# Reordered first units, earlier weight loads, regrouped first output pieces and filler matmuls in a recurrence + soft-MoE kernel

## The chip, the cores and the metric

The kernel runs on one core of one Trainium2 chip. The metric is the device time of one execution in microseconds (us); the median of 13 runs of the kernel before is 205.56 us. Times inside an execution come from one profiled run and are counted from the start of its span.

## What is computed

The input is a sequence tensor of 4 batches, 5056 steps and 256 channels. First a gated linear recurrence runs over the steps of each batch; then a soft mixture of experts (MoE) with 8 experts of 4 slots each mixes all 20224 tokens. Cut to what matters:

```python
sig = 1.0 / (1.0 + np.exp(-f_logit))
f = lower_bound + (1.0 - lower_bound) * sig
for t in range(S):                       # per batch and channel
    h = f[:, t] * h + (1.0 - f[:, t]) * x[:, t]
    y[:, t] = h
# y becomes x of shape (20224, 256)
logits = x @ phi                         # 32 slots
d = softmax of logits over tokens;  slot_input = d.T @ x
for e in range(8):                       # w1: 256 x 1024, w2: 1024 x 256
    slot_out[e] = np.maximum(slot_input[e] @ w1[e], 0.0) @ w2[e]
c = softmax of logits over slots;  out = c @ slot_out
```

So nothing can be written out before the last step of the recurrence has fed the slots and all expert weights have been used.

## The kernel before, in words

**Units.** The work is cut into 40 units: 10 groups of 512 steps times 4 batches, unit n being group n // 4 of batch n % 4. The load of a unit is 512 KB of `f_logit` and 512 KB of `x`, both float32. The expert weights are 16 further loads (8 of w1, 8 of w2), cast to bf16 on the way, issued one by one by `load_w` (L118) from GpSimd's queue; L120 is w1, L122 is w2. In the profile all of these weight tiles are called w_sb.

**Stages of a unit.** `load` (L162) puts f and x of a unit into buffers of the pool `ld`, which holds three pairs of units of each. `gate` (L180) is the sigmoid on ScalarE, f_t to s_t (L188). `enter` (L190) multiplies s_t and x_t into u_t on GpSimd (L199; unit 0 on VectorE, L195). `s_to_channels` and `u_to_channels` (L216, L222) transpose both on TensorE into PSUM tiles sp and up (L214; L208 and L211 in the odd group 8). `decay` (L230) turns sp into the factors a on ScalarE (L237). `scan` (L241) is the recurrence on VectorE, two instructions of L247 per unit. `to_tokens` (L252) transposes h back (L258, tile hp), and `keep_tokens` (L268) copies it to ht (L272), on VectorE for even n and on ScalarE for odd n. Per group, `logits`, `exps` (with two activation table loads), `weights_to_tokens` and `slots` follow.

**Order.** The scheduler is off (`tc.manual_schedule()`, L132): every engine executes its instructions in the order in which the Python program emits them, and waits in place for what it needs. The main loop (L408) runs n from 0 to 39 and emits stages of several units per step: in the first units (n < 4) the gate of unit n+3, the decay of n+2, and the scan of n; from n = 4 on, on even n, the gate of n+4 and n+5 in one instruction, and on odd n the decay of n+1 and n+2. `W_AT` (L130) is a table from n to the number of weight loads emitted in that step, right after `enter(n + 3)` on GpSimd.

**Limits on buffers.** sp has one PSUM buffer (a pair of units), hp one, up two. A transpose into sp for the next pair waits for the decays of the pair before; `to_tokens(n)` waits for `keep_tokens(n - 1)`, and what is behind it on TensorE waits too. A load waits until its buffer has been read by the gate (f) or by enter (x).

**The experts.** When the slots are summed, sin (L521, L522) goes through w1 (L539), Relu, a transpose, and w2. Experts 0 to 3 share one pass (L575). Experts 4 to 7 are the loop over j at L583: eight matmuls (L585) each, which need the weights w2[4 + j]; after j = 0, the earlier experts' sum is added (L590) and the row sums of groups 4 to 9 are taken (L319, L322) into one half of a PSUM tile called tail. Four reciprocals (L598) follow in VectorE's order, then slot_out (L599). `spin(dst, k)` (L125) emits k matmuls of 512 columns whose result nobody uses; the kernel before has seven of them elsewhere.

**The output.** Each of 41 output units (40, and one for the odd ends of group 8) is made of matmuls into a PSUM tile op (L622), a scaling into ob by VectorE (`by_vector`, L628) or ScalarE (`by_scalar`, L633), and a write issued from SyncE's queue. op has four row blocks of 256 float32[...]. The first two units are split over both engines (L646 to L652): unit 0 into four pieces of 128 KB, unit 1 into two of 256 KB; the others are written whole (L660).

Of the kernel before, what the change touches and what calls it, by code (L numbers as in the profile page):

```python
# [18 lines left out]
def kernel(  # L19
# [10 lines left out]
    nc = tc.nc  # L30
# [8 lines left out]
    R = 4  # L39
    G = P * R  # L40
    n_grp = (S + G - 1) // G
    n_unit = n_grp * B
# [84 lines left out]
            nc.tensor.matmul(dst, w1_sb[0][:, 0, :P], w1_sb[0][:, 0, :G],  # L127
                             start=True, stop=True, skip_group_check=True)

    W_AT = {12: 1, 18: 1, 24: 1, 29: 1, 32: 1, 33: 1, 34: 3, 35: 1, 36: 6}  # L130
    w_next = [0]
    ctx.enter_context(tc.manual_schedule())  # L132

# [4 lines left out]
    with tc.tile_pool(name="sp2", bufs=3) as sp2, \  # L138
# [203 lines left out]
        def unit(f, m):  # L342
            if 0 <= m < n_unit:
                f(m)
# [45 lines left out]
        SINGLE, AHEAD = 6, 6  # L390
# [11 lines left out]
        enter(1)  # L402
        s_to_channels(1)
        u_to_channels(1)
        decay(1, 1)
        gate(2, 1)
        enter(2)
        for n in range(n_unit):  # L408
            if n < SINGLE - 2:
                if n:  # L410
                    unit(u_to_channels, n + 1)
                    unit(to_tokens, n - 1)
                s_to_channels(n + 2)
                decay(n + 2, 1)
                if n + 3 < SINGLE:
                    gate(n + 3, 1)
                else:
                    gate(n + 3)
                if n % 2 == 0:
                    unit(load, n + AHEAD)  # L420
                unit(enter, n + 3)
            else:
                end = n >= n_unit - 6
                if n % 2 == 0:
                    unit(load, n + AHEAD)
                    if not end:
                        unit(gate, n + 4)
                else:
                    unit(decay, n + 1)
                    if n == n_unit - 5:  # L430
                        gate(n + 3)
                        exps(odd - 1)
                if not end and n != n_unit - 7:
                    group(exps, n - 2)

                unit(enter, n + 3)
                for _ in range(W_AT.get(n, 0)):
                    load_w(w_next[0])
                    w_next[0] += 1

                if n == n_unit - 2:
                    unit(u_to_channels, n + 1)
                unit(to_tokens, n - 1)
                if n == n_unit - 2:
                    keep_tokens(n - 1)
                if n % 2 == 0:
                    unit(s_to_channels, n + 2)
                    unit(s_to_channels, n + 3)
                if n != n_unit - 2:
                    unit(u_to_channels, n + 1)  # L450
                if n in (n_unit - 5, n_unit - 4):
                    idle(4)
                if n == n_unit - 2:
                    tail = psp.tile([P, 2, G], F32, name="tail", tag="sp")
                    rs_ps = tail[:, 0, ds(0, n_grp * R * B)].rearrange(
                        "p (g r b) -> p g r b", r=R, b=B)
                    late_ps, odd_ps = (
                        tail[:, 1].bitcast(BF16)[:, ds(i * R * P, R * P)].rearrange(
                            "p (r s) -> p r s", r=R) for i in range(2))
                    logits(odd)  # L460
                    exps(odd)
                    left_over()
                    slots(odd - 1)
                    spin(tail[:, 1], 1)
                    odd_weights()
                elif not end:
                    group(logits, n - 1)
            if n == n_unit - 1:
                logits(last, [0, 1, 2])
                late_exps([0, 1, 2])  # L470
                for g in range(4):
                    row_sums(g)
                late_weights([0, 1, 2], nc.scalar.copy)

            unit(scan, n)
            if n == 0:
                rep_constants()
            if n != n_unit - 2:
                unit(keep_tokens, n - 1)
            if n == n_unit - 3:  # L480
                weights_to_tokens(odd - 1)
                slots(odd - 2)
            elif not n >= n_unit - 6:
                group(weights_to_tokens, n - 3)
                batch(slots, n - 4, 0)
                batch(slots, n - 4, 1)
# [26 lines left out]
    with tc.tile_pool(name="ew", bufs=1) as ew, \  # L513
# [15 lines left out]
        Q = 4  # L529
# [20 lines left out]
        for q in range(E // Q):  # L550
# [4 lines left out]
            if q == 0:  # L555
# [4 lines left out]
                dst = hid[:, :, :, ds(0, SPE)]  # L560
# [22 lines left out]
        for j in range(Q):  # L583
            for fc in range(FC):
                nc.tensor.matmul(so_ps, wide[:, fc, j].rearrange("p b s -> p (b s)"),  # L585
                                 w2_sb[Q + j][:, fc],
                                 start=j == 0 and fc == 0, stop=j == Q - 1 and fc == FC - 1,
                                 skip_group_check=True)
            if j == 0:
                nc.tensor.matmul(so_ps, rep2, so4, start=False, stop=False,  # L590
                                 skip_group_check=True)
                for g in range(4, n_grp):
                    row_sums(g)
        for part, ps in ((rrow[:, 4:odd], rs_ps[:, 4:odd]),
                         (rrow[:, odd, ds(0, R3)], rs_ps[:, odd, ds(0, R3)]),
                         (rrow[:, odd, R3, ds(0, B // 2)], rs_ps[:, odd, R3, ds(0, B // 2)]),
                         (rrow[:, last], rs_ps[:, last])):
            nc.vector.reciprocal(part, ps)  # L598
# [4 lines left out]
    with tc.tile_pool(name="pout", bufs=4, space=PSUM) as pout, \  # L603
# [4 lines left out]
        for n, (g, b) in enumerate(units):  # L608
            n_r = B // 2 if b is None else part_rows(g)
            op = pout.tile([P, R, D], F32, name="op", tag="op")  # L610
            ob = osb.tile([P, R, D], F32, name="ob", tag="ob")
            if b is None:
                for j in range(n_r):
                    k = ds(j * 2 * NS, 2 * NS)
                    nc.tensor.matmul(op[:, j * R // n_r], left[k].rearrange("s t u -> s (t u)"),
                                     slot_out[k, :], start=True, stop=True,
                                     skip_group_check=True)
                scale = rrow[:, odd, R3, ds(0, n_r)].unsqueeze(2)
            else:
                ew = etall[:, ds(g * G, P * n_r)].rearrange("s (p r) -> s p r", r=n_r)  # L620
                for r in range(n_r):
                    nc.tensor.matmul(op[:, r], ew[ds(b * NS, NS), :, r],  # L622
                                     slot_out[ds(b * NS, NS), :],
                                     start=True, stop=True, skip_group_check=True)
                scale = rrow[:, g, ds(0, n_r), ds(b, 1)]

            def by_vector(r, k):
                nc.vector.tensor_tensor(ob[:, ds(r, k)], op[:, ds(r, k)],  # L628
                                        scale[:, ds(r, k)].broadcast_to([P, k, D]), ALU.mult)

            def by_scalar(r0, k):
                for r in range(r0, r0 + k):
                    nc.scalar.activation(ob[:, r], op[:, r], ACT.Copy, scale=scale[:, r])  # L633

            if b is None:
                nc.vector.tensor_tensor(
                    ob[:, ds(0, n_r)], op.rearrange("p (j k) d -> p k j d", j=n_r)[:, 0],
                    scale.broadcast_to([P, n_r, D]), ALU.mult)
                load_dve += 0.6
                for j in range(n_r):  # L640
                    dst = out.rearrange("(b t) d -> t b d", b=B)
                    nc.sync.dma_start(
                        out=dst[ds(first(odd) + P * R3, L), ds(2 * j, 2)], in_=ob[:, j])
                continue
            dst = out[ds(b * S + first(g), P * n_r)].rearrange("(p r) d -> p r d", r=n_r)
            if n < 2:  # L646
                k = 1 if n == 0 else R // 2
                for r in range(0, R, 2 * k):
                    by_vector(r, k)
                    nc.sync.dma_start(out=dst[:, ds(r, k)], in_=ob[:, ds(r, k)])  # L650
                    by_scalar(r + k, k)
                    nc.sync.dma_start(out=dst[:, ds(r + k, k)], in_=ob[:, ds(r + k, k)])  # L652
                continue
            if load_dve + 1.2 <= load_act + 1.8:
                load_dve += 1.2 * n_r / R
                by_vector(0, n_r)
            else:
                load_act += 1.8 * n_r / R
                by_scalar(0, n_r)
            nc.sync.dma_start(out=dst, in_=ob[:, :n_r])  # L660
# [30 lines left out]
```

## Time and profile before

| What | Value |
|---|---|
| Median of 13 runs | 205.56 us (205.42 to 206.87) |
| The profiled execution's own time | 205.73 us |
| Its span | 204.0 us |
| VectorE busy | 145.7 us (71%) |
| TensorE busy | 135.1 us (66%) |
| ScalarE busy | 134.1 us (66%) |
| GpSimd busy | 98.9 us (48%) |
| Read from HBM | 58.23 MB |
| Written to HBM | 20.71 MB |
| Mean rate moved by the DMA engines | 347 GB/s |

The profiled time is 1.73 us more than its span and 0.17 us above the median. Rates of weight loads count the bf16 bytes that arrive, half of the float32 bytes read.

### The profile page before, as it was taken

What the parts mean: (1) busy time and instruction counts of PE and PEld (TensorE: products, weight loads), DVE (VectorE), ACT (ScalarE), POOL (GpSimd) and SP (SyncE); (2) the same over time, 40 slices, a digit from 0 to 9 for tenths busy, and PEclk for the clock granted to TensorE, in tenths of its full rate; (3) what the DMA queues carried; (4) which work ended last, traced back from release to release, by engine and by line L of the source; (5) the groups of instructions that cost most, each with busy time, mean ns of one, the idle gap of its engine ahead of it and who ended that gap; (6) DMA issues with size and microseconds to landing.
All of it is one profiled execution on the core that took longest, in us unless ns stands there. A gap on an engine that the chain in (4) does not pass through costs nothing.

```text
span 204.0 us, 3127 instructions
## 1 busy us (share of the span) xinstructions
PE 135.1 (66%) x1097; PEld 93.9 (46%) x1097; DVE 145.7 (71%) x166; ACT 134.1 (66%) x182; POOL 98.9 (48%) x70
## 2 busy tenths in 40 slices
PE   0557558575967767585976767999647678776700
PEld 0336345555756646564765646548522223321300
DVE  1686549979997999979999999543283656645540
ACT  2666698879996999879988595622074354564240
POOL 2564849982998469981996959910000000000000
PEclk9999978789996999969999999999985555555555
DMA  5999999999999999999999999999269999999995
GB/s 175 411 410 411 409 410 406 411 410 407 410 317 407 414 311 417 412 346 370 399 397 328 292 221 215 213 213 216 51 228 398 406 407 406 407 406 407 402 383 222
DMA packets 21215, 70.75 MB, mean 347 GB/s; under 512 B 2496, under 2 KB 3776, under 8 KB 21200
## 3 DMA queue, kind: packets, MB, share of 16 engines
q1 hardware_dynamic: 18720, 62.14, 77.3%
q0 software_dynamic: 2336, 8.42, 20.5%
q8 instruction: 8, 0.13, 0.3%
q14 instruction: 7, 0.06, 0.1%
q10 hardware_dynamic: 144, 0.00, 0.0%
HBM read 58.23 MB, written 20.71 MB: 387 GB/s over the span
## 4 chain that ended last, share of the span: by engine, by line
DMA 29%; DVE 28%; PE 15%; ACT 11%; issue 9%; POOL 4%; SPq 1%; DVEq 0%; ACTq 0%; POOLq 0%
DVE h L247 20%; DMA out_dram<-ob 18%; DMA w_sb<-in_moe_w_dram 9%; PE sp L214 6%; ACT s_t L188 5%; PE hp L258 4%; DVE ht L272 4%; ACT a L237 3%; POOL u_t L199 3%; DVE ob L628 3%; ACT ob L633 2%; PE up L214 2%; DMA f_t<-in_f_logit_dram 2%; POOL w_sb L122 2%; DVE et L310 1%
## 5 line engine op out<-in xcount | busy, mean ns | idle before, releaser
L199 POOL TENSOR_TENSOR u_t<-s_t,x_t 128x1024 bf16<-128x1024 bf16 (+1 forms) x39 | 82.1, 2128 | 29.1 <-ACT s_t L188 20.2
L247 DVE TENSOR_TENSOR_SCAN h<-a,h,up 128x512 bf16<-128x512 f32 (+1 forms) x72 | 86.2, 1250 | 6.7 <-PE up L214 3.6
L237 ACT ACTIVATE a<-sp,nomlb 128x1024 f32<-128x1024 bf16 (+2 forms) x46 | 43.5, 997 | 12.6 <-PE sp L214 11.5
L258 PE MATMUL hp<-ident_f,h 128*128 128x128 f32 (+1 forms) x160 | 30.4, 315 | 26.9 <-DVE ht L272 17.6
L633 ACT ACTIVATE ob<-op,rrow 128x256 f32<-128x256 f32 x63 | 24.7, 477 | 31.1 <-DVE ob L628 23.0
L628 DVE TENSOR_TENSOR ob<-op,rrow 128x1024 f32<-128x1024 f32 (+3 forms) x26 | 28.4, 1110 | 20.4 <-DMA out_dram<-ob 17.4
L622 PE MATMUL op<-slot_out,etall 32*128 32x256 bf16 x156 | 32.3, 379 | 14.1 <-ACT ob L633 10.1
L188 ACT ACTIVATE s_t<-f_t 128x2048 bf16<-128x2048 f32 (+2 forms) x23 | 38.4, 1674 | 3.4 <-DMA f_t<-in_f_logit_dram 3.3
L258 PEld LDWEIGHTS hp<-ident_f,h 128*128 128x128 f32 (+1 forms) x160 | 22.8, 207 | 37.1 <-DVE ht L272 21.9
L214 PE MATMUL sp<-ident_f,s_t 128*128 128x128 f32 x144 | 24.4, 320 | 10.5 <-ACT s_t L188 9.3
L622 PEld LDWEIGHTS <-etall 32*128 32x128 bf16 x156 | 14.0, 122 | 32.0 <-issue 28.3
L214 PE MATMUL up<-ident_f,u_t 128*128 128x128 f32 x144 | 25.2, 302 | 3.9 <-POOL u_t L199 3.9
L214 PEld LDWEIGHTS sp<-ident_f,s_t 128*128 128x128 f32 x144 | 20.1, 166 | 11.9 <-issue 6.1
L214 PEld LDWEIGHTS up<-ident_f,u_t 128*128 128x128 f32 x144 | 19.0, 157 | 6.1 <-POOL u_t L199 5.3
L272 DVE COPY ht<-hp 128x512 f32<-128x512 f32 (+1 forms) x20 | 13.4, 669 | 4.5 <-PE hp L258 4.5
L272 ACT COPY ht<-hp 128x512 f32<-128x512 f32 (+1 forms) x20 | 11.7, 587 | 6.7 <-PE hp L258 6.7
L247 DVE TENSOR_TENSOR_SCAN h<-a,up 128x512 bf16<-128x512 f32 x8 | 9.2, 1205 | 1.2 <-PE up L214 1.2
L286 PE MATMUL lg<-h,phi 128*32 128x512 bf16 (+1 forms) x80 | 7.7, 434 | 0.0
L336 PE MATMUL slot_ps<-ht,et 128*32 128x256 bf16 (+1 forms) x144 | 5.5, 273 | 0.8 <-DVE et L310 0.8
L188 ACT ACT_TABLE_LOAD x4 | 5.1, 1283 | 1.2 <-PEq L675 1.2
L295 ACT ACT_TABLE_LOAD x4 | 5.1, 1283 | 0.1
L585 PE MATMUL so_ps<-w_sb,wide 128*128 128x256 bf16 x32 | 4.0, 273 | 1.2 <-DMA w_sb<-in_moe_w_dram 1.2
(88 smaller groups left out, 84.8 us busy)
## 6 DMA issues: line engine op xcount, KB each, us to landing
f_t<-in_f_logit_dram SPq DMA_DIRECT2D x36, 512.0 KB, 9.9
x_t<-in_x_dram SPq DMA_DIRECT2D x36, 512.0 KB, 9.5
out_dram<-ob SPq DMA_DIRECT2D x34, 512.0 KB, 5.9
w_sb<-in_moe_w_dram POOLq DMA_DIRECT2D x16, 512.0 KB, 9.0
f_t<-in_f_logit_dram SPq DMA_DIRECT2D x4, 384.0 KB, 8.8
x_t<-in_x_dram SPq DMA_DIRECT2D x4, 384.0 KB, 8.0
out_dram<-ob SPq DMA_DIRECT2D x4, 384.0 KB, 4.9
out_dram<-ob SPq DMA_DIRECT2D x6, 128.0 KB, 2.2
```

Of the source, the lines that this page charges most:

```text
L188: nc.scalar.activation(s_t, f_t, ACT.Sigmoid, scale=-1.0)
L199: nc.gpsimd.tensor_tensor(uts[n][:, :r], s_t[:, :r], x_t[:, :r], ALU.mult)
L214: nc.tensor.transpose(ps[:, :, r], t[:, r], ident_f)
L237: nc.scalar.activation(decays[n // 2, o][:, ds(n % 2, k), :T], sp[:, ds(n % 2, k), :T, o], ACT.Identity, scale=nomlb[:, ds(o, 1)], bias=1.0)
L247: nc.vector.tensor_tensor_scan(h[:, :T, o], decays[n // 2, o][:, n % 2, :T], up[:, :T, o], hs[n - B][:, ds(used(n // B - 1) - 1, 1), o] if ...
L258: nc.tensor.transpose(hp[:n_p, r], hw[:, :n_p, r], ident_f)
L272: copy(hts[g][:n_p, b].rearrange("p r d -> p (r d)").bitcast(F32), hps.pop(n)[:n_p].rearrange("p r c -> p (r c)"))
L286: nc.tensor.matmul(lg[ds(b * NS, NS), :], phi[:, o], hs[g * B + b][:, :T, o], start=o == 0, stop=o == DC - 1, skip_group_check=True)
L336: nc.tensor.matmul(slot_ps[ds(b * NS, NS), :], et[:n_p, r, b], ht[:n_p, b, r], start=(g == 0 and r == 0), stop=(g == n_grp - 1 and r == R ...
L622: nc.tensor.matmul(op[:, r], ew[ds(b * NS, NS), :, r], slot_out[ds(b * NS, NS), :], start=True, stop=True, skip_group_check=True)
L628: nc.vector.tensor_tensor(ob[:, ds(r, k)], op[:, ds(r, k)], scale[:, ds(r, k)].broadcast_to([P, k, D]), ALU.mult)
L633: nc.scalar.activation(ob[:, r], op[:, r], ACT.Copy, scale=scale[:, r])
```

## The change

There are four edits.

1. **First units.** Before the loop, gate(2) is emitted ahead of decay(1). For n of 0 to 2, the gate of unit n+3 comes ahead of the decay of n+2; for n of 1 to 3, to_tokens(n-1) comes ahead of u_to_channels(n+1). At n = 4, to_tokens(3) and keep_tokens(3) come ahead of the gate of units 8 and 9.
2. **Weight loads.** The first, second and third come three steps earlier, the fourth two, the fifth one. The others stay.
3. **First output pieces.** Unit 0 is emitted as block 0 on VectorE, 2 on ScalarE, 1 on VectorE, 3 on ScalarE, in place of 0, 1, 2, 3. For unit 1 the order stays as it was.
4. **Fillers.** Four `spin` matmuls follow experts j = 0, 1 and 2, after the row sums for j = 0. They write the half of tail that the row sums don't use.

```diff
-    W_AT = {12: 1, 18: 1, 24: 1, 29: 1, 32: 1, 33: 1, 34: 3, 35: 1, 36: 6}
+    W_AT = {9: 1, 15: 1, 21: 1, 27: 1, 31: 1, 33: 1, 34: 3, 35: 1, 36: 6}
...
+        gate(2, 1)
         decay(1, 1)
-        gate(2, 1)
         enter(2)
         for n in range(n_unit):
             if n < SINGLE - 2:
                 if n:
+                    unit(to_tokens, n - 1)
                     unit(u_to_channels, n + 1)
-                    unit(to_tokens, n - 1)
                 s_to_channels(n + 2)
-                decay(n + 2, 1)
                 if n + 3 < SINGLE:
                     gate(n + 3, 1)
+                    decay(n + 2, 1)
                 else:
+                    decay(n + 2, 1)
                     gate(n + 3)
...
                     unit(load, n + AHEAD)
+                    if n == SINGLE - 2:
+                        to_tokens(n - 1)
+                        keep_tokens(n - 1)
                     if not end:
                         unit(gate, n + 4)
...
-                unit(to_tokens, n - 1)
+                if n != SINGLE - 2:
+                    unit(to_tokens, n - 1)
...
-            if n != n_unit - 2:
+            if n not in (SINGLE - 2, n_unit - 2):
                 unit(keep_tokens, n - 1)
...
                 for g in range(4, n_grp):
                     row_sums(g)
+            if j < Q - 1:
+                spin(tail[:, 1], 4)
...
-                for r in range(0, R, 2 * k):
-                    by_vector(r, k)
-                    nc.sync.dma_start(out=dst[:, ds(r, k)], in_=ob[:, ds(r, k)])
-                    by_scalar(r + k, k)
-                    nc.sync.dma_start(out=dst[:, ds(r + k, k)], in_=ob[:, ds(r + k, k)])
+                for r in range(0, R // 2, k):
+                    for by, i in ((by_vector, r), (by_scalar, r + R // 2)):
+                        by(i, k)
+                        nc.sync.dma_start(out=dst[:, ds(i, k)], in_=ob[:, ds(i, k)])
```

## The prediction

> **What bounds the kernel now.** I read the forty slices first, then the chain of work that ended last, then the timeline around the places that the change touches.
>
> ```profile
> DMA  5999999999999999999999999999269999999995
> GB/s 175 411 410 411 409 410 406 411 410 407 410 317 407 414 311 417 412 346 370 399 397 328 292 221 215 213 213 216 51 228 398 406 407 406 407 406 407 402 383 222
> ```
>
> A slice is 5.1 us. The DMA engines are full from the second slice to the 28th. Slices near 213 GB/s are no slack: they hold weights, counted at half of what is read. As a check, 58.23 MB read over 2.7 to 144.3 us is 411 GB/s, the rate of the pure loads. So no order of loads ends the reads earlier; only the bytes ahead of one load can change. Then come a gap and a write stage full at about 406 GB/s.
>
> ```profile
> 124.66 2.58 POOL w_sb L122 x5
> 127.24 18.31 DMA w_sb<-in_moe_w_dram
> 145.60 1.05 PE so_ps L585 x8
> 146.67 0.49 DVE slot_out L599
> ```
>
> In the chain (start, us, what) the end is set by the last weight, w2[7], through the matmuls of j = 3 and slot_out; the writes follow. Arithmetic comes close behind:
>
> ```profile
> 127.60 0.39 PE L127 MATMUL tail<-w_sb 128*128 128x512 bf16 x1
> 133.50 0.82 PE L127 MATMUL tail<-w_sb 128*128 128x512 bf16 x3
> 142.48 1.91 PE L585 MATMUL so_ps<-w_sb,wide 128*128 128x256 bf16 x16
> 145.60 1.03 PE L585 MATMUL so_ps<-w_sb,wide 128*128 128x256 bf16 x8 [1.21 <-DMA w_sb<-in_moe_w_dram]
> ```
>
> The reader is to see that j = 1 and 2 run back to back from 142.48, waiting for no weight (w2[5] and w2[6] land at 140.6 and 143.1), and that TensorE's only wait is 1.21 us ahead of j = 3. One matmul takes (0.82 - 0.39)/2 = 0.213 us at 512 columns; at 256, with one of 0.273 us latency, (1.91 - 0.273)/15 = 0.109 us. So the sixteen are issued by 142.48 + 16 x 0.109 = 144.23, and the slack is 145.60 - 144.23 = **1.37 us**.
>
> [...] the trace has the granted clock at 1.00 in every microsecond from 142 to 151. [...] with a weight in flight, 58 to 60 us moved 270 GB/s, which by the two rates (410 and 210) is 30% for the loads and 70% for the weight. [...]
>
> **Edit 4, fillers.** Twelve matmuls at 0.213 us are 2.56 us on TensorE, all in series ahead of j = 3; 1.37 us of it fits into its wait. The rest, **1.19 us, goes onto the end**: j = 3 would start at 146.79. Nothing is won against it, as the clock is already full there. The reciprocals of L598 come later in program order, and in the built program they wait for the last filler, because it writes the tile (tail) that they read. They take 0.82 us beside the 1.03 us of j = 3: estimate 0, at most 0.1.
>
> **Edit 3, first pieces.**
>
> ```profile
> 147.84 0.42 DVE L628 TENSOR_TENSOR ob<-op,rrow 128x256 f32<-128x256 f32 x1 [0.68 <-PE op L622]
> 148.34 0.47 ACT L633 ACTIVATE ob<-op,rrow 128x256 f32<-128x256 f32 x1 [7.96 <-DVE ob L628]
> 148.85 3.29 DVE L628 TENSOR_TENSOR ob<-op,rrow 128x256 f32<-128x256 f32 x4 [0.59 <-ACT ob L633]
> 149.31 2.90 ACT L633 ACTIVATE ob<-op,rrow 128x256 f32<-128x256 f32 x7 [0.49 <-DVE ob L628]
> ```
>
> VectorE and ScalarE alternate strictly, and VectorE's second piece (block 2) waited for ScalarE's (block 1)[...]. So the waits go by tile. In the built changed program the four pieces have the same waits: ScalarE's first on VectorE's first, VectorE's second on ScalarE's first, and so on. I take **0**. If they did overlap, SyncE would issue the four writes at 148.39, 148.79, 149.22 and 149.68 (its own 0.35 to 0.41 us each, and 0.05 between), not the last at 149.81: 0.13 us won. Bounds 0 to -0.15.
>
> **Edit 1, first units.** By the timeline, gate, transpose and decay follow each other with nothing between: s_t starts at 11.84, 15.26, 19.18 and 22.14. ScalarE's own work is 1.06 + 1.27 = 2.33 us a unit, so the gate no longer waits for a transpose. What ends the gain is the loads.
>
> ```profile
> 28.06 1.58 PE L214 MATMUL sp<-ident_f,s_t 128*128 128x128 f32 x8 [2.06 <-ACT s_t L188]
> 30.58 2.45 DVE L247 TENSOR_TENSOR_SCAN h<-a,h,up 128x512 bf16<-128x512 f32 x2 [3.03 <-ACT ht L272]
> 38.29 1.91 ACT L188 ACTIVATE s_t<-f_t 128x2048 bf16<-128x2048 f32 x1 [0.84 <-DMA f_t<-in_f_logit_dram]
> ```
>
> Followed by hand, with each row's own time and the landings of the loads (f6 and f7 about 21.6, f8 and f9 about 26.8, f10 and f11 about 31.6): the gate of 6 and 7 starts at 23.8, not 26.10, and the scan of unit 5 at 28.05, not 30.58, a lead of 2.5 us. But the gate of 12 and 13 waits for its load already before, at 38.29, and a full DMA won't bring it sooner. Behind it, the decay of 10 and 11 gains only its 1.17 us wait for TensorE (41.88 to about 40.7). Scan 12 needs ScalarE's copy of unit 9, so **1.1 us** of lead is left there. Adverse end: to_tokens now stands ahead of u_to_channels and waits for the copy of two units before, which I included; cost to the lead up to 0.4.
>
> **Edit 2, weights.** Five loads trade places with data loads in a full stream: no byte less, and none of the last eleven moves. GpSimd issues as many (about 0.6 us each, between enters). For units between the old and the new place, loads come later, by up to a whole weight (2.45 us: 1.05 MB read at 428 GB/s, as the last six land 2.45 us apart). Most have room: f18 and f19 land at 52.7 for a gate at 56.3, f22 and f23 at 66.4 for 71.08. One has none:
>
> ```profile
> 84.35 1.91 ACT L188 ACTIVATE s_t<-f_t 128x2048 bf16<-128x2048 f32 x1
> 85.91 0.57 POOL L120 DMA_DIRECT2D w_sb<-in_moe_w_dram  x1
> 86.70 0.59 ACT L272 COPY ht<-hp 128x512 f32<-128x512 f32 x1 [0.44 <-PE hp L258]
> 88.46 2.12 ACT L237 ACTIVATE a<-sp,nomlb 128x1024 f32<-128x1024 bf16 x2 [1.17 <-PE sp L214]
> ```
>
> f29 lands at 84.2, and its gate starts at 84.35. The third weight, issued at 85.91, would now be issued at about 78.4 and flow from about 82.0 (3.6 us after issue, as for the first). The last 1.2 us of f29 then runs at a share of 30 to 50%: 1.2 to 2.8 us late; I take 1.8. The gate ends at 87.9, and ScalarE's copy, queued behind it, at 88.5 instead of 87.3; behind that come the decay and TensorE's hp. With ScalarE's own waits (0.44 + 1.17) as cushion, the lead falls from 1.1 to between 0 and 0.6: I take **0.3**. From 98 to 130 us VectorE is full, so the lead stays. f36 and f37, later by the fourth weight, cost about 1 us of ScalarE, which then waited 2.05 us for hp anyway. x39 landed at 121.0 for an enter at 122.49, room for 1.5 us of lead.
>
> **The sum.** Every microsecond of lead moves sin (135.5) and j = 1 earlier, and the weights not at all. Change = max(0, 1.19 - lead) = 1.19 - 0.3 = +0.89, with edits 2 and 3 adding nothing else. The profiled run goes from 205.73 to 206.62, its span from 204.0 to 204.9; that run is 0.17 above the median, so the median goes from 205.56 to **206.45**.
>
> **The rivals.**
> *The lead survives (not slower).* The fillers are free once the lead reaches 1.19 us, for j = 3 then waits for w2[7] as before. For it: a lead of 1.1 at unit 12, and GpSimd needs to issue the third weight only 1 us later to miss f29. Against: the gate's margin of 0.15 us. Time 205.56 + 0.09 = 205.65, within 0.2% (0.41 us, about what a measurement of this kernel can tell from no change).
> *The lead turns negative.* f29 late by a whole weight, or colder TensorE stretches in front: lead -0.5, change +1.7, 207.25.
> *Faster.* The read stream ends raggedly: from 143 to 145 the DMA share is 0.69 and 0.39, so 0.92 us of capacity is unused. If other places of the weights even that out and the lead covers the fillers, up to 0.9 is won: 204.7. It takes both.
>
> **How the numbers follow.** Forecast (lead -0.3 to 0.7): 0.52. Lead survives: 0.27, nearly all of it within 0.2%. Negative lead: 0.11. Faster: 0.10. So slower by over 0.2% is 0.52 + 0.11 + 0.02 = 0.65, within 0.2% is 0.24, faster 0.11 with a scrap of the second case. The range runs from 205.25 (lead survives, less edit 3's 0.15 and its own spread) to 207.1 (lead about -0.35), which leaves out most of the faster case and part of the negative one.
>
> **What would show it.** Twelve more L127 matmuls of 0.213 us apart after 142; no wait for w_sb ahead of the last eight L585, which start near 146.5; w2[7] still landing near 145.5; alternating ob pieces with unchanged gaps; scan 5 near 28; and a wait for f_t of about 2.5 us ahead of the gate near 84 to 86. I am wrong if j = 3 still waits for the weight, or if the weight lands more than 0.5 us from 145.5.

## The result, and the profile after

The changed kernel takes **209.67 us** (median of 11 runs, 207.69 to 210.76), the kernel before 205.62 us (48 runs in all): a ratio of 1.018 [1.016, 1.021]. It is slower, by more than four times what was forecast: 4.05 us against 0.89. The profiled execution took 209.48 us, its span 207.7 us.

The forty slices of the changed kernel, the same two rows as before:

```profile
DMA  5999999999999999999999999997069999999985
GB/s 192 411 414 406 413 408 409 407 400 325 417 410 320 412 413 408 317 410 397 371 346 334 289 214 213 214 211 147 2 213 405 404 405 408 408 405 405 400 330 216
```

Full to the same point. The gap between reads and writes is now a slice at 2 GB/s (before: 51), and the next at 213 (228). The loss lies between the last read and the point where the writes flow.

The chain that ended last, where it passes the experts (start, us, what):

```profile
142.96 0.88 PE tail L127 x4
...
147.32 0.89 PE so_ps L590 x8
```

The last weight has gone out of it: fillers and matmuls of the experts follow each other. The timeline there:

```profile
142.82 1.02 PE L127 MATMUL tail<-w_sb 128*128 128x512 bf16 x4
...
143.68 1.04 PE L590 MATMUL so_ps<-w_sb,wide 128*128 128x256 bf16 x8
...
145.42 1.04 PE L590 MATMUL so_ps<-w_sb,wide 128*128 128x256 bf16 x8
...
147.15 1.04 PE L590 MATMUL so_ps<-w_sb,wide 128*128 128x256 bf16 x8
147.35 0.82 DVE L605 RECIPROCAL rrow<-tail 128x64 f32<-128x64 f32 x4 [6.05 <-PE tail L127]
```

The groups for j = 1, 2 and 3 start 1.74 and 1.73 us apart, and the last has no wait: 147.15 against 145.60 before, **1.55 us later**. The reciprocals run beside it and hold up nobody.

The output's first pieces keep their old pattern:

```profile
149.39 0.42 DVE L635 TENSOR_TENSOR ob<-op,rrow 128x256 f32<-128x256 f32 x1 [0.68 <-PE op L629]
149.90 0.47 ACT L640 ACTIVATE ob<-op,rrow 128x256 f32<-128x256 f32 x1 [9.18 <-DVE ob L635]
...
150.41 1.02 DVE L635 TENSOR_TENSOR ob<-op,rrow 128x256 f32<-128x256 f32 x2 [0.59 <-ACT ob L640]
```

So far everything is 1.55 us late and no more. The rest comes with the writes. SyncE's queue (start, us, what), in the kernel before and then in the changed one:

```profile
150.92 0.44 SPq L652 DMA_DIRECT2D out_dram<-ob  x1
151.40 4.98 SPq L660 DMA_DIRECT2D out_dram<-ob  x5
```

```profile
152.33 2.21 SPq L658 DMA_DIRECT2D out_dram<-ob  x1
154.58 0.43 SPq L666 DMA_DIRECT2D out_dram<-ob  x1
```

The sixth write, of 256 KB, takes 2.21 us to issue; the median of the first six writes is 0.41, and before they took 0.35 to 0.59. The whole units start at 154.58, not 151.40: 3.18 us late, 1.55 of it from the experts and **1.6 from this one issue**. Meanwhile the DMA engines run dry (stretch, then busy time by engine, TensorE's clock, DMA share, GB/s):

```profile
153.00:154.00 1.00, 0.81 (x8) 0.31 (x6) 1.00 (x2) 0.77 (x3) 0.00 (x0) 0.50 0.46 174
154.00:155.00 1.00, 0.99 (x9) 0.48 (x6) 0.82 (x1) 0.00 (x0) 0.00 (x0) 0.50 0.06 12
```

A share of 0.06 is as much as one engine of sixteen. What came just ahead of it stands among the DMA queues of 152.0 to 152.5 us (packets, MB, share of 16 engines in the stretch):

```profile
q1 hardware_dynamic: 145, 0.13, 78.3%
q8 instruction: 1, 0.02, 22.4%
```

A packet of the queue that the profile calls "instruction", taken here for an instruction fetch. It has 16 KB (the page of the kernel before has eight in 0.13 MB), is counted whole where it starts (the 0.05 us from 152.35 show 224.1%), and comes to 0.224 x 16 x 0.5 = 1.8 us of one engine's time, in the middle of the first pieces. The kernel before has such a packet too, at 154.3, which is 5.9 us after its first write was issued; by then several whole units have been issued, and its DMA share stays up, at 1.05:

```profile
154.00:155.00 1.00, 1.00 (x8) 0.44 (x5) 0.63 (x1) 0.19 (x1) 0.00 (x0) 0.50 1.05 401
```

In the changed kernel the packet comes 2.4 us after the first write, and it starts, at 152.35, with the long issue (152.33).

The 0.5 us still missing from the 3.7 by which the spans differ lies after 154.58. At its first whole unit the changed kernel has an empty DMA (0.06), the kernel before a full one (0.95), which fits but wasn't tested.

### Whose fetch it is

The trace doesn't name the engine that fetches. The packets on q8, and the TensorE records (matmuls and weight loads), point to it:

| | q8 packets, us | TensorE records between them |
|---|---|---|
| before | 33.8, 55.7, 77.2, 98.1, 114.8, 131.6, 142.4, 154.3 | 304, 244, 270, 243, 295, 329, 146 |
| after | 31.3, 55.7, 77.3, 98.4, 115.0, 131.9, 142.6, **152.3**, 198.2 | 301, 246, 263, 240, 295, 322, 135, 276 |

Single gaps differ, from 135 to 329, but the mean is about 260 before, while VectorE, ScalarE and GpSimd have 166, 182 and 70 records in the whole kernel. The count of records from the start is steadier: up to the eighth packet, 1999 of TensorE before and 1980 after, and 1993, 1971, 1981 and 1990 in four runs below (edits 1 to 3 alone; after with 24 and before with 36 small matmuls at the start; two tiles), although that packet's time goes from 154.3 to 146.1 us. So I take q8 for TensorE's, which is inferred. The twelve fillers are 24 records with their weight loads (1109 of each on the page, 1097 before), and all stand ahead of the packet at 152.3. The runs below bear it out, as matmuls added on TensorE alone move the packet ahead: to 152.3 us with 12 at the start of the kernel before, 147.9 with 24 and 146.4 with 36. A second instruction queue, q14, can be left aside: it has two packets of 8 KB between 148.2 and 151.4 us before and after, and at like places in the runs without a long issue.

### The profile page after: what moved, and what is told of

Its sections match the earlier page's. It is cut to its first block, busy times and chain, and to the rows that moved or that the text cites. A ratio compares the mean times of both kernels' runs of the same rounds, so it can differ in the third digit from the quotient of the medians.

```text
span 207.7 us, 3150 instructions
## 1 busy us (share of the span) xinstructions
PE 138.4 (67%) x1109; PEld 95.4 (46%) x1109; DVE 147.9 (71%) x166; ACT 134.8 (65%) x182; POOL 99.2 (48%) x70
## 4 chain that ended last, share of the span: by engine, by line
DMA 30%; DVE 28%; PE 20%; issue 7%; SPq 6%; ACT 4%; DVEq 0%; ACTq 0%
DVE h L247 18%; DMA out_dram<-ob 12%; DMA f_t<-in_f_logit_dram 11%; DMA x_t<-in_x_dram 7%; SPq L666 6%; DVE ob L635 5%; DVE ht L272 4%; PE hp L258 3%; PE sp L214 3%; PE up L214 2%; PE tail L127 2%; PE so_ps L590 2%; PE slot_ps L336 1%; PE hi_ps L544 1%; DVE et L310 1%
## 5 line engine op out<-in xcount | busy, mean ns | idle before, releaser
L258 PE MATMUL hp<-ident_f,h 128*128 128x128 f32 (+1 forms) x160 | 31.1, 321 | 31.2 <-DVE ht L272 17.6
L629 PE MATMUL op<-slot_out,etall 32*128 32x256 bf16 x156 | 33.7, 388 | 13.4 <-ACT ob L640 10.8
L214 PE MATMUL sp<-ident_f,s_t 128*128 128x128 f32 x144 | 23.7, 314 | 9.2 <-ACT s_t L188 8.0
L214 PE MATMUL up<-ident_f,u_t 128*128 128x128 f32 x144 | 25.1, 302 | 0.8 <-POOL u_t L199 0.8
L214 PEld LDWEIGHTS sp<-ident_f,s_t 128*128 128x128 f32 x144 | 19.5, 163 | 10.7 <-issue 5.7
L214 PEld LDWEIGHTS up<-ident_f,u_t 128*128 128x128 f32 x144 | 19.3, 158 | 2.2 <-POOL u_t L199 1.2
L286 PE MATMUL lg<-h,phi 128*32 128x512 bf16 (+1 forms) x80 | 7.2, 403 | 0.0
L336 PE MATMUL slot_ps<-ht,et 128*32 128x256 bf16 (+1 forms) x144 | 6.0, 289 | 0.8 <-DVE et L310 0.8
L605 DVE RECIPROCAL rrow<-tail 128x64 f32<-128x64 f32 (+3 forms) x4 | 0.8, 268 | 6.0 <-PE tail L127 6.0
```

The source lines that it names most:

```text
L214: nc.tensor.transpose(ps[:, :, r], t[:, r], ident_f)
L258: nc.tensor.transpose(hp[:n_p, r], hw[:, :n_p, r], ident_f)
L336: nc.tensor.matmul(slot_ps[ds(b * NS, NS), :], et[:n_p, r, b], ht[:n_p, b, r], start=(g == 0 and r == 0), stop=(g == n_grp - 1 and r == R ...
L629: nc.tensor.matmul(op[:, r], ew[ds(b * NS, NS), :, r], slot_out[ds(b * NS, NS), :], start=True, stop=True, skip_group_check=True)
```

## The experiments

All medians stand against 205.62 to 205.66 us of the kernel before on the same chips.

| Kernel | Median, us | Ratio to before | Profiled run, us | First write | q8 packet from it | Longest of the first six issues |
|---|---|---|---|---|---|---|
| before | 205.62 | 1 | 205.73 | 148.39 | +5.9 | 0.59 |
| after | 209.67 | 1.018 [1.016, 1.021] | 209.48 | 149.95 | +2.4 | 2.21 |
| edits 1 to 3 alone | 205.78 | 1.001 [1.000, 1.003] | 205.31 | 147.95 | +5.8 | 0.45 |
| edit 4 alone | 209.13 | 1.019 [1.016, 1.021] | 209.13 | 149.74 | +2.5 | 2.19 |
| before, 12 small matmuls late | 207.71 | 1.010 [1.008, 1.013] | 208.58 | 149.31 | +2.4 | 2.09 |
| after, 24 small matmuls late | 208.16 | 1.012 [1.010, 1.014] | 208.48 | 151.05 | -3.8 | 0.53 |
| before, 12 at the start | 207.46 | 1.008 [1.006, 1.011] | 207.76 | 149.13 | +3.2 | 0.63 |
| before, 24 at the start | 206.72 | 1.006 [1.003, 1.008] | 206.54 | 147.98 | -0.1 | 1.29 |
| after, 24 at the start | 207.39 | 1.007 [1.005, 1.010] | 207.37 | 149.86 | -3.5 | 0.61 |
| edits 1 to 3, 10 matmuls at n = 11 | 206.06 | 1.001 [0.999, 1.003] | 205.47 | 148.16 | +3.7 | 0.46 |
| edits 1 to 3, 26 matmuls at n = 11 | 206.68 | 1.004 [1.002, 1.007] | 208.14 | 149.95 | -0.2 | 0.84 |
| one filler, 33 at the start | 206.38 | 1.003 [1.001, 1.005] | 205.54 | 148.03 | -1.8 | 0.46 |
| before, 36 at the start | 206.05 | 1.001 [0.999, 1.004] | 205.61 | 148.08 | -1.7 | 0.45 |
| the same, first unit on two tiles | 205.06 | 0.996 [0.995, 0.998] | 204.89 | 147.69 | -1.5 | 0.44 |

The last four columns are of the profiled run (in the last row the issues are SyncE's four). An issue of more than 1 us stands only where the packet falls 2.4 to 2.5 us behind the first write or right beside it (-0.1). In the three longest cases issue and packet begin within 0.1 us of each other: 152.33 and 152.35, 152.15 and 152.22, 151.72 and 151.72.

### Which edit

The changed kernel without the fillers:

```diff
-            if j < Q - 1:
-                spin(tail[:, 1], 4)
```

> The changed kernel without edit 4: no filler matmuls; edits 1, 2 and 3 stay. Theory A (the loss is edit 4 alone, in two parts: 1.5 us of matmuls in series, and 2.2 us of output writes held up because the 24 further TensorE instructions move an instruction fetch into the first output writes): the last expert starts when its weight lands, near 145.5, the writes have no hole, and the time is 205.6, within 0.3 of the kernel before. Rival B (the hole in the writes comes from edit 3, the new order of the first pieces): the hole near 153 to 155 stays, and the time is near 207.8. Rival C (the reordered front or the earlier weights cost time at the end): over 206.2 with the last weight landing late.

205.78 us, 1.0012 [0.9996, 1.0029]: nothing that the measurement can tell. Its last group waits for the weight again:

```profile
145.16 1.03 PE L590 MATMUL so_ps<-w_sb,wide 128*128 128x256 bf16 x8 [0.41 <-DMA w_sb<-in_moe_w_dram]
```

And the fillers put into the kernel before, at the same place:

```diff
+            if j < Q - 1:
+                spin(tail[:, 1], 4)
```

> The kernel before with edit 4 alone: four filler matmuls after each of the experts j = 0, 1, 2. Theory A: 1.2 us in series (2.56 less the 1.37 of slack) and the hole in the first writes, 2.2 us: 205.6 + 3.4 = 209.0. Rival B: the series part alone, 206.8, and no hole. Rival C: also 206.8.

209.13 us, with j = 3 at 146.94 (+1.34) and the same long issue:

```profile
152.15 2.19 SPq L654 DMA_DIRECT2D out_dram<-ob  x1
```

The fillers make the whole loss, 3.51 us without the other edits; edits 1 to 3 make none that can be told. And the fillers cost more than they keep TensorE busy, 2.56 us.

### Fillers' time or fetch

To part the two, matmuls were added whose own time costs the end little. First ahead of unit 30's step, twelve of 16 columns into an unused PSUM half:

```diff
+                if n == 30:
+                    for _ in range(12):
+                        nc.tensor.matmul(slot_bank[:, 1, :16], w1_sb[0][:, 0, :P],
+                                         w1_sb[0][:, 0, :16], start=False, stop=False,
+                                         skip_group_check=True)
```

> The kernel before with 12 further matmuls of 16 columns in step n = 30 of the main loop, whose result nobody uses. They are 24 instructions on TensorE, as many as the fillers, but some 0.5 us long in all and 40 us ahead of the end, where TensorE has time to spare. Theory A, its second part: the fetch that stood near 154 comes into the first writes as in the changed kernel, SyncE's issue is held up near 152, and the time is about 207.7 although no arithmetic is on the path. Rival (the hole depends on the late fillers themselves, on their time or the clock, or on edit 3): 205.6, no hole.

207.71 us, as expected, but the run parts nothing cleanly: in its profiled execution, of 208.58 us, j = 1 started at 144.77, 2.3 us late, and the cause lies ahead of the added matmuls (scan 5 at 32.11 instead of 30.58; the last section comes back to it). The long issue is there, 2.09 us from 151.72. The same in the changed kernel, 24 of them:

```diff
+                if n == 30:
+                    for _ in range(24):
...
```

> The changed kernel with 24 further matmuls of 16 columns in step n = 30, 48 more instructions on TensorE, whose result nobody uses. Theory A: the fetch moves from 152.2 to before the first write (about 147 to 149, when the DMA engines are idle), the hole goes, and the time falls to 205.6 + 1.5 = 207.2, although the kernel does more. Rival (the hole does not hang on the fetch's place): 209.7 or more.

The packet moved to 147.3, ahead of the first write, and the hole was gone, as expected; but 208.16 us is 1.0 more than forecast, since j = 3 came at 148.25, 1.1 us later than in the changed kernel. Whether the added matmuls (0.75 us from 105.74) did that isn't shown: the scan behind them is on time (108.98, changed kernel 109.36), and only the one after it is late, as it is in a run below that has none of them. The next went ahead of everything, of 4 columns:

```diff
+        for _ in range(12):
+            nc.tensor.matmul(slot_bank[:B, 1, :B], ones, ones, start=True, stop=True,
+                             skip_group_check=True)
         lb_constants()
         gate(0, 1)
```

> The kernel before with 12 further matmuls of 4 columns on TensorE ahead of everything else, where it has nothing to do for 6 us; their result isn't used. 24 instructions, as many as the fillers, and no time on the path. Theory A (the place of an instruction fetch decides): last weight and last expert as before (145.5, 145.6), first write near 148.4, a fetch near 150.7 (2.3 us after the first write, as with the fillers), SyncE held up for some 2 us, a hole of 1.5 to 2 us: 207.3. Rival (the hole needs the late fillers or a late chain): 205.6, no hole.

207.46 us, near the forecast, but not in the way that was forecast. The packet is at +3.2, when the whole units are already being issued (from 152.19), the longest of the first six issues is 0.63 us, and the DMA share of 151 to 155 us is 0.66, 0.93, 0.57 and 0.89: capacity lost in two places, not one hole. 0.74 us of the loss is the chain's (first write at 149.13). That the time fits is luck as far as this trace shows. With 24:

```diff
+        for _ in range(24):
...
```

> The same with 24 such matmuls, 48 instructions. Theory A: the fetch falls ahead of the first write, no hole, 205.6, and fewer single runs near 207 than before has. Rival that more instructions cost as such: more than with 12.

A miss: 206.72, not 205.6. The packet landed beside the first write. SyncE's second issue is the long one, and the DMA share of 148 to 151 us is 0.12, 0.31 and 0.66:

```profile
148.43 1.29 SPq L655 DMA_DIRECT2D out_dram<-ob  x1
```

Moving the packet by twelve matmuls more was not enough to clear the writes. The clearest test is the changed kernel, fillers and all, with the same 24 at the start:

```diff
+        for _ in range(24):
...
         lb_constants()
```

> The changed kernel with 24 such matmuls ahead of everything. Theory A: the fetch falls ahead of the first write, which stays near 150; no hole; the time is that of the fillers' series part alone, 205.6 + 1.5 = 207.2. Rival: 209.7.

**207.39 us, 2.28 us faster than the changed kernel with 24 matmuls more to do.** The first write stays where it was (149.86 against 149.95) and j = 3 too (147.06 against 147.15); the packet starts at 146.3, six issues take 2.99 us together, and the whole units start at 152.89:

```profile
149.86 2.99 SPq L661 DMA_DIRECT2D out_dram<-ob  x6
152.89 1.13 SPq L669 DMA_DIRECT2D out_dram<-ob  x2
```

Five of its six runs took 206.67 to 207.54 us and one 209.88; of the changed kernel's eleven, one took 207.69 and the others 209.01 to 210.76. So the 4.05 us split into 2.28 for the place of the fetch and 1.77 for the rest, of which 1.55 is j = 3's. That the place of the fetch decides is shown, by this run and by the last two columns of the table. Why SyncE's issue takes 2.2 us beside a packet of 1.8 was not shown.

### Where the lead went

In the changed kernel scan 5 starts at 28.41 (before: 30.58) and scan 11 at 46.58 (48.75): a lead of 2.17 us. Scan 12 has 0.62 left, scan 13 none:

```profile
48.99 1.12 PE L258 MATMUL hp<-ident_f,h 128*128 128x128 f32 x4 [3.06 <-ACT ht L272]
...
51.07 2.45 DVE L247 TENSOR_TENSOR_SCAN h<-a,h,up 128x512 bf16<-128x512 f32 x2 [0.23 <-PE up L214]
54.10 2.46 DVE L247 TENSOR_TENSOR_SCAN h<-a,h,up 128x512 bf16<-128x512 f32 x2 [0.58 <-PE up L214]
```

TensorE waits 3.06 us for ScalarE's copy, which stands behind a gate and two table loads, and its four transposes then take 1.12 us, not 0.75. The stretch after it (PE, PEld, DVE, ACT, POOL, then the granted clock):

```profile
50.00:52.00 2.00, 2.00 (x22) 1.14 (x21) 1.62 (x2) 1.99 (x2) 2.00 (x2) 0.50 1.01 410
```

Half clock, where the kernel before, with a wait of 2.08 us at the same place, has 1.00:

```profile
50.00:52.00 2.00, 1.82 (x25) 1.44 (x26) 2.00 (x4) 2.00 (x3) 2.00 (x2) 1.00 1.03 410
```

The gate near 84, the one that the prediction made late, starts at 84.52 without a wait: with no lead left, the third weight is issued at 79.70, not 78.4. To test the clock's part, matmuls of 256 columns into the unused half of slot_bank were put into that wait, in the kernel without fillers, first ten, in the step of n = 11:

```diff
+                if n == 11:
+                    for _ in range(10):
+                        nc.tensor.matmul(slot_bank[:, 1], ident, etall[:, :D],
+                                         start=True, stop=True, skip_group_check=True)
                 if n != SINGLE - 2:
                     unit(to_tokens, n - 1)
```

> Edits 1, 2 and 3 without the fillers, and ten matmuls of 256 columns ahead of to_tokens(10) in step n = 11, whose result isn't used. They break up the 3.06 us in which TensorE waited for ScalarE's copy in the changed kernel, after which it ran at half clock to 52.8 and the lead of the front went from 2.2 us (scan 11) to nothing (scan 13). Theory (the half clock ate the lead): TensorE stays at full clock from 46 to 54, scan 13 starts near 53, 1 us earlier than in the changed kernel, and the one of unit 14 near 56. Rival (the buffers and ScalarE alone set it): scan 13 at 54.1 as before. The 20 further instructions may move the fetch into the first writes; so the lead is read from the trace, not from the time.

206.06 us, 1.0009 [0.9987, 1.0030]: inconclusive. The wait shrank to 1.86 us, the clock was still at 0.50 from 50 to 52, and scan 13 started at 54.17. So 26 of them:

```diff
+                    for _ in range(26):
...
```

> As the run with ten matmuls ahead of to_tokens(10), but with 26 of them, 2.8 us, so that TensorE has next to no idle time before the copy of unit 9. With ten, the clock still fell to half at 49.8. Theory (the half clock ate the lead): full clock from 46 to 56, scan 12 near 50.4, scan 13 near 53.0, scan 14 near 56.0, 1 us ahead of the kernel before (56.97), and the last weight again what j = 3 waits for. Rival (ScalarE and the copies alone set the pace): scan 14 near 57.0 at full clock too. The time is within 1 us of 205.6 either way, as the last weight sets the end; 52 further instructions move the fetch near the first write, which can cost up to 1 us.

Now the clock stays at 1.00 and the lead lives on: scan 12 starts at 50.32 (before: 51.69) and scan 14 at 55.64 (56.97), 1.3 us ahead. And then the step on f29 appears where the prediction had it:

```profile
86.36 1.91 ACT L188 ACTIVATE s_t<-f_t 128x2048 bf16<-128x2048 f32 x1 [1.87 <-DMA f_t<-in_f_logit_dram]
```

The load of f29, in place at 84.2 before, holds the gate until 86.36: 2.1 us later, a wait of 1.87 us. (The 1.8 in the prediction was the author's estimate, for a share of 30 to 50%; 58 to 60 us of the kernel before give the 30, and the 50 no trace shows.) The lead is gone by 99 us. The median is 206.68 us, 1.0043 [1.0015, 1.0072], no faster. The profiled execution took 208.14 us, 1.5 more than the median: in it j = 1 starts 2.9 us late (145.36 against 142.48), and the q8 packet lies at 149.8, beside the first write at 149.95. That the half clock took the lead in the changed kernel is shown, as the transposes behind the wait start at 48.92 us with ten matmuls and with 26, and the lead goes at half clock and stays at full clock; what makes this run late after 99 us stays open.

### What might do better

One filler an expert fits into the slack of 1.37 us (3 x 0.213 = 0.64), and 33 small matmuls at the start make 36 in all, to get the packet ahead of the writes:

```diff
-                spin(tail[:, 1], 4)
+                spin(tail[:, 1], 1)
...
+        for _ in range(33):
+            nc.tensor.matmul(slot_bank[:B, 1, :B], ones, ones, start=True, stop=True,
+                             skip_group_check=True)
```

> The changed kernel with one filler in place of four after each of the experts, and 33 matmuls of 4 columns ahead of everything, so that it has 72 more TensorE instructions than before and the fetch falls some 3 to 4 us ahead of the first write. Theory: three fillers are 0.64 us, less than the slack of 1.0 to 1.37; j = 3 waits for its weight, and the time is 205.6 to 205.9. Rival (a filler costs more than its matmul, or the fetch isn't what holds the writes up): 206.3 or more.

The profiled run took 205.54 us, below the forecast, with j = 3 at 145.24, the first write at 148.03 and no hole. The median is 206.38 (22 runs, 205.43 to 208.12), a miss by 0.5 us and where the rival had it; the trace shows one run and not what spreads them. As its control, the kernel before with 36 such matmuls at the start:

```diff
+        for _ in range(36):
...
         lb_constants()
```

> The kernel before with 36 matmuls of 4 columns ahead of everything, 72 more TensorE instructions. Theory: the fetch falls some 3 to 4 us ahead of the first write, as in the changed kernel with 24 such matmuls; no hole, 205.6, where 24 instructions gave 207.5 and 48 gave 206.7 with it near the first write. Rival (each added instruction costs): over 207.5.

206.05 us, 1.0014 [0.9993, 1.0035], 0.45 more than forecast: no gain from moving the fetch ahead of the writes, where it had never been in the way. On top of it, a first unit for which edit 3's idea takes effect: two PSUM tiles and two buffers, ScalarE's half written from ScalarE's own queue:

```diff
+                if n == 0:
+                    op2 = pout.tile([P, R, D], F32, name="op2", tag="op")
+                    ob2 = osb.tile([P, R, D], F32, name="ob2", tag="ob")
...
+            if n == 0:
+                for r in range(2):
+                    for by, q, o, t in ((nc.vector, nc.sync, op, ob), (nc.scalar, nc.scalar, op2, ob2)):
+                        if by is nc.vector:
+                            nc.vector.tensor_tensor(t[:, ds(r, 1)], o[:, ds(r, 1)],
+                                                    scale[:, ds(r, 1)].broadcast_to([P, 1, D]),
+                                                    ALU.mult)
+                            nc.sync.dma_start(out=dst[:, ds(r, 1)], in_=t[:, ds(r, 1)])
+                        else:
+                            nc.scalar.activation(t[:, r], o[:, r], ACT.Copy, scale=scale[:, 2 + r])
+                            nc.scalar.dma_start(out=dst[:, ds(2 + r, 1)], in_=t[:, ds(r, 1)])
+                continue
```

> The kernel before with the 36 matmuls ahead of everything, and the first output unit split over two PSUM tiles and two buffers: blocks 0 and 1 by VectorE, written from SyncE's queue, blocks 2 and 3 by ScalarE, written from its own queue. What edit 3 is named for is then really done. Theory (the waits go by tile): the four pieces overlap, VectorE's two back to back from 147.8 and ScalarE's from 147.9, and SyncE's issue of the whole units starts about 0.9 us earlier than at 151.40: 204.8. Rival (SyncE's or the DMA engines' own pace sets it): 205.6.

**205.06 us, 0.9962 [0.9946, 0.9978]**: faster than both kernels. VectorE's two pieces run back to back and ScalarE's beside them:

```profile
147.13 0.76 DVE L657 TENSOR_TENSOR ob<-op,rrow 128x256 f32<-128x256 f32 x2 [0.46 <-PE op L628]
147.40 0.47 ACT L662 ACTIVATE ob<-op,rrow 128x256 f32<-128x256 f32 x1 [6.49 <-PE op L628]
147.69 0.82 SPq L660 DMA_DIRECT2D out_dram<-ob  x2
```

ScalarE starts when TensorE's block is done, not when VectorE is, and the whole units start at 150.43 instead of 151.40 before and 150.93 in the control. About half of the 1.0 us is thus not this change's, and the change is three in one, a second op, a second ob and a second queue, whose shares in the gain aren't parted. The overlap itself is shown: ScalarE's first piece, 147.40 to 147.87, lies within VectorE's two, 147.13 to 147.89.

## Why the prediction was wrong, step by step

- **The failed step: edit 4 as arithmetic alone.** "Twelve matmuls at 0.213 us are 2.56 us on TensorE" is right, and so is the 1.19 us that doesn't fit into the slack. What the sum, "The rest, 1.19 us, goes onto the end", lacks is that the fillers are also 24 more instructions, with which the q8 packet comes 2.4 us behind the first write and not 5.9 (1.6 of it because that write comes later), and one issue beside it takes 2.21 us. The prediction put this at nothing without looking at it. Moving the fetch away is worth 2.28 us (24 small matmuls at the start of the changed kernel). None of the rivals had it.
- **The lead's size.** "I take 0.3"; measured at the end -0.34 (sin at 135.87 against 135.53). Series and lead give 1.19 + 0.34 = 1.53 for the 1.55 by which j = 3 is late. That is near the rival of the negative lead. The sign is less sure than the sum makes it look: these are single executions, and the kernel before with 36 and with 24 matmuls at the start has sin at 135.72 and 136.27.
- **The lead's cause.** "The lead falls" at f29: not here. It was gone at scan 13 (54.1 us), through the half clock after a wait that edit 1 makes longer (3.06 against 2.08 us). The rival's "colder TensorE stretches in front" named this cause. The prediction followed the first units by hand and was close (28.41 for scan 5, where 28.05 was forecast), but gave every TensorE row the time that it had before. The step on f29 was no error in itself: with the lead kept alive, the wait of 1.87 us is there, and two runs without it have part of it (0.94 us with ten matmuls at n = 11, 0.61 us with the fillers and 24 matmuls at the start).
- **"From 98 to 130 us VectorE is full, so the lead stays"** was not tried, as no lead came that far.
- **Edit 3: right.** Alternation and gaps are unchanged, 0 us. The run with two tiles shows that sharing op and ob, which it splits together, was what held it back.
- **Edit 2: right for the end.** Without fillers the last group starts at 145.16 after its wait for the weight, 0.34 from the 145.5 forecast; edits 1 to 3 together cost nothing that can be told.
- **The reciprocals: right.** They run at 147.35 to 148.17, while j = 3 lasts to 148.19.
- **Two slips that change nothing.** (0.82 - 0.39)/2 is 0.215, not 0.213, 0.02 us more for the twelve; and the reads run on to 145 us (DMA share 0.29 from 144.5), not 144.3, 409 GB/s instead of 411.

In the sum, of the 3.75 us between the two profiled runs, 1.19 was priced rightly, 0.34 stands where -0.30 was taken, and some 2.2 was missing.

## What to carry to other kernels

Twelve matmuls cost this kernel their time and also moved a packet: at 2.4 us behind the first write it stood beside an issue of 2.21 us, at 5.9 beside none of more than 0.59. So after adding or removing instructions, look where the packets on the "instruction" queue now fall, above all among the first writes. If a change looks dearer than its busy time, add a few idle instructions early in the program: here 24 small matmuls made the changed kernel 2.28 us faster. Then the fetch is the first suspect, and the packet's new place and the issue times have to agree. And follow an engine's waits too when a chain is moved forward: here a wait of 3.06 us and not 2.08 was followed by a clock of 0.50 and not 1.00, and four transposes took 1.12 us and not 0.75.

## What the hardware showed that had not been expected

- One 16 KB packet took 1.8 us among the first writes, and SyncE's issue beside it 2.2 us (median of the first six 0.41). With the DMA engines idle such a packet took 0.93 us (at 146.3, changed kernel with 24 matmuls at the start). Among the whole units, at 154.3 us in the kernel before, it took 1.37 us (42.9% of 16 engines in 0.2 us) and left no mark on the DMA share (1.05).
- TensorE's clock, near the copy of unit 9 at 49 us: in all five runs with a wait of 3.06 us it was halved (0.50 from 50 to 52 us in the changed kernel). Of eight waits of 1.86 to 2.54 us at this place, three were followed by half clock (1.86, 2.21 and 2.42) and five were not (1.90 twice, 1.97, 2.08 and 2.54). With ten matmuls at n = 11 a wait of 1.86 us was followed by 0.50, in the kernel before one of 2.08 by 1.00: the length of one wait doesn't decide here.
- Two medians differed by up to 0.8 us from profiled runs with the forecast trace (205.54 against 206.38, 205.61 against 206.05), and runs of the kernel before also reach 207.26. One difference between such runs is on record: the profiled run with 12 small matmuls late, whose program is the kernel before up to 108 us, has TensorE slow until 33 us. The same four transposes of h, in the kernel before and there:

```profile
25.25 0.75 PE L258 MATMUL hp<-ident_f,h 128*128 128x128 f32 x4 [0.35 <-DVE ht L272]
```

```profile
25.97 1.13 PE L258 MATMUL hp<-ident_f,h 128*128 128x128 f32 x4
```

Scan 5 is 1.5 us late there, and the scan at 106.03 us 2.3 (before: 103.72). The granted clock is shown as 1.00 in this stretch, as it is from 8 to 16 us in the kernel before, where a transposing matmul of L214 takes 0.42 us and not 0.27; so read the durations beside it. Whether this is what spreads the other runs stays open.
